# Attention with key-block summaries and a two-branch max layer: 128 key rows of one padded k per query tile, v loaded by token and spread by engine copies, max layer in units of 256 tokens

## The chip, the cores and the metric

The kernel runs on one core of a Trainium2 chip. The metric is the device time of one execution in microseconds (us); lower is better. The core has a matrix engine (TensorE, PE in the profile, with its weight loads as PEld), a vector engine (VectorE, DVE), a scalar engine (ScalarE, ACT), a general engine (GpSimd, POOL) and a queue that issues the transfers of this kernel (SyncE, SP). Matrix products land in PSUM, which has eight banks here; everything else lives in SBUF, 128 partitions wide.

## The reference

Four batches, eight heads, 768 tokens, head size 64. Each query sees the keys nearer than 16 tokens and, besides, 24 summaries of blocks of 32 tokens (key: the maximum over the block; value: the mean), all in one softmax. The result, 3072 tokens of width 512, goes through a layer that takes the larger of two projections and projects it back.

```python
def _attn_ref(q, k, v):
    ...
    k_sum = k.reshape(B, H, nb, block, D).max(axis=3)
    v_sum = v.reshape(B, H, nb, block, D).mean(axis=3)
    scores_l = scale * np.matmul(q, k.transpose(0, 1, 3, 2))
    mask_l = np.abs(pos[:, None] - pos[None, :]) < window
    scores_s = scale * np.einsum('bhsd,bhnd->bhsn', q, k_sum) + np.log(block)
    a = softmax(concat([where(mask_l, scores_l, -1e9), scores_s]))
    return a @ concat([v, v_sum])

def _moe_ref(x, w1, w2, w_out):
    g = np.maximum(x @ w1, x @ w2)
    return g @ w_out
```

(The two formulas are shortened here to what is computed.) The maximum is rewritten as x@w1 + relu(x@(w2−w1)), so the kernel needs the difference of the weights (`wd`), `w_out` (`wo`), and the product w1@w_out (`w1o`), which it makes once.

## The kernel before, in words

Queries are cut into 12 tiles of 64 tokens per batch. A tile sees a window of 96 keys (at most) and the 24 summaries: NK = 120 rows. Two heads are worked on at once (a head pair `hp`, four in a batch) and three groups `grp` of four tiles.

`load_batch` (L137) issues for each head pair one load of k, q and v, 384 KB each, in which a descriptor is 512 B (two tokens of one head). `load_weights` (L144) issues twelve loads of 512 KB. All transfers are issued from the SP queue, in its order; the stage tiles of k, q and v have three buffers each.

`prep_v` (L179) casts v to bf16 on DVE (L182, `vb`), then spreads it with 16 SBUF-to-SBUF transfers (L188 to L195) into `vext`, which holds for each tile the 96 value rows of its window, and makes the 24 means with six matmuls (L199, `vs_ps`), copies them once (L201) and repeats them over the tiles with one more transfer (L202). `prep_kq` (L207) casts k and q on DVE (L211, L213), transposes them on PE (L219), copies the windows of k on DVE (L231, L232), takes the block maxima (L234, `ks`), repeats them with one POOL copy (L236) into `kext`, and copies q on ACT (L242) into a block-diagonal `qbd`. `scores` (L246) does four matmuls (L253), an exponential on ACT (L255) into one of four `prob` buffers, and a mask product on DVE (L262). `values` (L266) does the matmuls with `vext` (L277) and, for every three tile pairs, a reciprocal (L282) and a product (L284) on DVE; the accumulator `av` has one PSUM buffer. `transpose_x` (L288) transposes the result (L294) and copies it on DVE (L296) into `xt`, in halves of 384 tokens.

`maxout` (L323) takes a half: eight hidden tiles of four matmuls with 384 columns (L330), a relu on ACT (L332), and three output tiles of twelve matmuls with 512 columns (L339, L343), an ACT copy (L347) and a store. The output accumulator `o_ps` has one PSUM buffer.

The program (L352 on) is: load batch 0, prepare its v, load the weights, attention of batch 0 alone, cast the weights (`cast_weights`, L157: `w1b` L160, `wd` L161 on DVE, `wo` L162 on ACT), make `w1o` (L164); then for each batch the max layer of batch b woven step by step with the attention of batch b+1. The order in which each engine and the SP queue take their instructions is not that of the text: the framework plans it ahead, instruction by instruction, from its own estimates of durations, the earlier in the text the sooner among what it takes to be ready. On the chip each engine then follows that fixed order, and waits wherever an instruction's operands are late.

The softmax here doesn't subtract the row's maximum and nothing guards it: scores larger than these inputs give would overflow.

## Time and profile before

| what | value |
|---|---|
| median of two runs | 225.51 us (224.62 and 226.40) |
| the profiled execution | 225.93 us, span 224.2 us |
| granted TensorE clock, mean | 0.985 |
| PE busy | 174.6 us (78%), 1475 matmuls |
| DVE busy | 118.0 us (53%) |
| ACT busy | 102.7 us (46%) |
| POOL busy | 23.9 us (11%) |
| transfers | 37.68 MB in 49858 packets |

The span is what the engines' records cover; the profiled execution's own time is 1.7 us longer. Busy shares are means over stages with different limits, so the profile is read by stretches of time: the start (load, attention of batch 0), the middle (max layer of one batch beside attention of the next), and the end (the max layer of batch 3 alone). In the lists, L is a line of the kernel printed above; a row of the list of groups gives the shapes as output<-input, a count, the busy time and the mean duration in ns.

### The profile page before, as it was taken

Reading aid. Unit: us, or ns where it says so; the run is one execution under the profiler, and the core shown is the slowest. Engines: PE = TensorE matmul, PEld = TensorE weight load, DVE = VectorE, ACT = ScalarE, POOL = GpSimd, SP = SyncE. Lnnn points to the kernel's source line nnn. Section 1 sums busy time; section 2 is a strip of 40 time slices with the busy share of each in tenths; the row PEclk is TensorE's granted clock in tenths of the full one; section 3 lists DMA queues with packets and bytes.
Section 4 is the critical chain, followed back from the end, with each engine's and each line's share of the span. In section 5 each row is a group of like instructions: output and inputs, shape, how many; then the busy total and the mean of one; then the engine's idle time right before and its main releaser. Section 6 shows DMA issues by size and latency. Waiting matters only on the chain.

```text
span 224.2 us, 3831 instructions
## 1 busy us (share of the span) xinstructions
PE 174.6 (78%) x1475; PEld 103.8 (46%) x1496; DVE 118.0 (53%) x268; ACT 102.7 (46%) x173; POOL 23.9 (11%) x61
## 2 busy tenths in 40 slices
PE   0003832665788999896989999999999999999973
PEld 0001622543553655664555466655546664544531
DVE  5432852899972950896857069844727853000000
ACT  2000651575120573585179248824935972442521
POOL 8990110000000010000011001000000000000000
PEclk9999999997699999999999999999999999999999
DMA  6998438999997335999634599634431101202112
GB/s 187 289 290 273 106 100 251 375 365 283 288 281 183 90 90 135 288 292 282 184 117 102 158 259 306 163 116 152 103 87 50 51 0 47 96 0 95 47 47 94
DMA packets 49858, 37.68 MB, mean 168 GB/s; under 512 B 2192, under 2 KB 44720, under 8 KB 49840
## 3 DMA queue, kind: packets, MB, share of 16 engines
q1 hardware_dynamic: 49840, 37.45, 58.5%
q8 instruction: 11, 0.18, 0.3%
q14 instruction: 7, 0.06, 0.1%
HBM read 25.17 MB, written 6.29 MB: 140 GB/s over the span
## 4 chain that ended last, share of the span: by engine, by line
PE 49%; DMA 15%; DVE 13%; ACT 11%; SPq 7%; issue 3%; POOL 1%; ACTq 0%; POOLq 0%
PE o_ps L343 16%; DMA vf<-in_v_dram 13%; PE h_ps L330 11%; PE o_ps L339 8%; PE av L277 4%; PE sc L253 2%; ACT g L332 2%; PE x_ps L294 2%; DMA vext_115<-vext_115 2%; DVE wd L161 2%; SPq L127 2%; ACT qbd_107 L242 2%; PE vs_ps L199 2%; ACT qbd_108 L242 2%; PE w1o_ps L174 2%
## 5 line engine op out<-in xcount | busy, mean ns | idle before, releaser
L330 PE MATMUL h_ps<-xt,wd 128*128 128x384 bf16 x256 | 54.2, 331 | 2.5 <-DVE xt L296 1.1
L343 PE MATMUL o_ps<-wo,g 128*128 128x512 bf16 x186 | 46.5, 379 | 0.3
L332 ACT ACTIVATE g<-h_ps 128x384 bf16<-128x384 f32 x64 | 30.1, 491 | 15.7 <-PE h_ps L330 15.2
L347 ACT COPY osb<-o_ps 128x512 f32<-128x512 f32 x24 | 14.1, 586 | 49.2 <-PE o_ps L343 49.1
L330 PEld LDWEIGHTS <-wd 128*128 128x128 bf16 x256 | 23.7, 98 | 16.8 <-issue 3.0
L343 PEld LDWEIGHTS <-g 128*128 128x128 bf16 x192 | 17.9, 98 | 18.2
L339 PE MATMUL o_ps<-w1o,xt 128*128 128x512 bf16 x83 | 24.1, 378 | 2.1 <-ACT osb L347 1.4
L199 PE MATMUL vs_ps<-vb_113,amean 128*128 128x512 bf16 x12 | 4.2, 502 | 20.4 <-DVE vb_113 L182 20.4
L282 DVE RECIPROCAL inv<-av 128x6 f32<-128x6 f32 x32 | 6.1, 190 | 25.0 <-PE av L277 24.9
L284 DVE TENSOR_TENSOR x<-av,inv 128x384 bf16<-128x384 f32 x32 | 17.6, 550 | 0.3
L234 DVE TENSOR_REDUCE ks<-k_ps 128x24 bf16<-128x768 bf16 x16 | 15.1, 945 | 0.0
L162 ACT CAST wo<-wof 128x1024 bf16<-128x1024 f32 x4 | 4.2, 1043 | 23.8 <-DMA wof<-in_moe_w_out_dram 23.8
L339 PEld LDWEIGHTS <-xt 128*128 128x128 bf16 x96 | 9.1, 97 | 10.4 <-issue 4.0
L199 PEld LDWEIGHTS <-amean 128*128 128x128 bf16 x24 | 2.5, 107 | 24.3 <-issue 13.8
L296 DVE COPY xt<-x_ps 128x384 bf16<-128x384 bf16 x32 | 11.3, 352 | 2.8 <-PE x_ps L294 2.2
L294 PE MATMUL x_ps<-identity,x 128*128 128x128 bf16 x96 | 11.2, 230 | 1.4 <-ACT qbd_108 L242 0.6
L242 ACT COPY qbd_107<-q_ps 64x768 bf16<-64x768 bf16 x10 | 7.9, 792 | 9.3 <-PE q_ps L219 9.2
L255 ACT ACTIVATE prob_109<-sc,bias 120x512 bf16<-120x512 f32 x12 | 8.3, 689 | 7.8 <-PE av L277 6.7
L242 ACT COPY qbd_106<-q_ps 64x768 bf16<-64x768 bf16 x12 | 9.5, 793 | 4.0 <-PE q_ps L219 3.9
L213 DVE CAST qb<-qf 128x768 bf16<-128x768 f32 x16 | 10.3, 647 | 1.1 <-DMA qf<-in_q_dram 1.1
L182 DVE CAST vb_113<-vf 128x768 bf16<-128x768 f32 x8 | 5.1, 638 | 10.4 <-DMA vf<-in_v_dram 10.3
L219 PE MATMUL k_ps<-identity,kb 128*128 128x128 bf16 x96 | 9.8, 236 | 1.0 <-DVE ks L234 0.9
(94 smaller groups left out, 251.0 us busy)
## 6 DMA issues: line engine op xcount, KB each, us to landing
kf<-in_k_dram SPq DMA_DIRECT2D x16, 384.0 KB
qf<-in_q_dram SPq DMA_DIRECT2D x16, 384.0 KB
vf<-in_v_dram SPq DMA_DIRECT2D x16, 384.0 KB
out_dram<-osb SPq DMA_DIRECT2D x24, 256.0 KB
w1f<-in_moe_w_dram SPq DMA_DIRECT2D x4, 512.0 KB
wof<-in_moe_w_out_dram SPq DMA_DIRECT2D x4, 512.0 KB
w2f<-in_moe_w_dram SPq DMA_DIRECT2D x4, 512.0 KB
vext_115<-vb_113 SPq DMA_DIRECT2D x8, 148.5 KB
```

Of the source, the lines that this page charges most:

```text
L199: nc.tensor.matmul(out=ps[:], lhsT=amean[:, c, :], rhs=vbt[:, c, j, :, 0:D], start=(c == 0 and j == 0), stop=(c == 2 and j == 1))
L213: nc.vector.tensor_copy(out=qb[:], in_=by_slot(loads["qf", b, hp]))
L234: nc.vector.tensor_reduce(out=ks[:], in_=kps.rearrange("p j (n g) -> p n j g", g=16), axis=AX.XY, op=ALU.max)
L242: nc.scalar.copy(out=qx[r, :, a * 64:a * 64 + 64].rearrange("p t (g j) -> p t g j", j=2), in_=qps[r].rearrange("p j (t g) -> p t g j", g=32))
L284: nc.vector.tensor_tensor(out=x[:], in0=av[:, :, :, 0:D], in1=inv[:].to_broadcast([128, 3, 2, D]), op=ALU.mult)
L294: nc.tensor.transpose(out=ps[:, u, :], in_=xs[half][:, u].rearrange("p a d -> p (a d)"), identity=identity[:])
L296: nc.vector.tensor_copy(out=xts[b, half][:, hp, :], in_=ps[:].rearrange("p u n -> p (u n)"))
L330: nc.tensor.matmul(out=h[:], lhsT=wd[:, c, f * 128:f * 128 + 128], rhs=xt[:, c, :], start=(c == 0), stop=(c == KC - 1))
L332: nc.scalar.activation(out=g[:, f, :], in_=h[:], func=ACT.Relu)
L339: nc.tensor.matmul(out=ps[:], lhsT=xt[:, c, sl], rhs=w1o[:, c, :], start=(c == 0), stop=False)
L343: nc.tensor.matmul(out=ps[:], lhsT=g[:, f, sl], rhs=wo[:, f, :], start=False, stop=(f == FC - 1))
L347: nc.scalar.copy(out=o[:, u, :], in_=ps[:])
```

## The change

The mask rows are rearranged and the geometry is made uniform. k is kept once per head pair as a padded row of 96 columns per tile (64 keys, 24 maxima, 8 zeros), and a tile's matmul reads 128 columns of it: its own 96 and the first 32 of the next tile. So K is 128 in place of 120 and one mask of 64 columns serves all tiles. `qbd` is laid out by head instead of by tile.

v is loaded by token: ten transfers per batch, with descriptors of 256 B (one token of one head), into one f32 tile `vf` with 128 tokens to a row block; it is cast into one bf16 tile `vb` (on POOL), and eight engine copies (on DVE in batch 0, on POOL later) spread it to `vext`, with a shift of partitions. The means are seven matmuls; the copy over the tiles is a DVE copy in batch 0 and a transfer later. The copy of the maxima goes from POOL to DVE.

The max layer works on three groups of 256 tokens in place of two halves of 384: four relu's of 512 columns per group, and one PSUM tag `mm` with two buffers for hidden and output tiles; `av` gets two buffers, `prob` nine. The transposes of the attention result are done for two head pairs at once. Weights are loaded in halves of the hidden width, w1 and w2 ahead of the loads of batch 1, w_out among them. For batch 0 there are an own attention (`first_attention`: casts of k on POOL and of q on ACT for head pairs 1 to 3, casts on DVE for k of pair 0, a third of the mask products on POOL) and an own max layer (`first_maxout`: half of the hidden tiles first, then the w1 transposes and `w1o`), which is woven with the attention of batch 1. `pin` keeps the marked instructions in program order.

```diff
-    NK = 96 + nb
...
+    NG, GT = 3, 256
+    KW = 96 * NT + 32
+    NV, VW = 7, 66
+    NBUF, NPB, WFB = 3, 9, 8
...
-    kext = [const.tile([128, NT, 128], BF16, name=f"kext{i}") for i in range(NBUF)]
-    qbd = [const.tile([128, NT, 128], BF16, name=f"qbd{i}") for i in range(NBUF)]
-    NPB = 4
-    prob = [const.tile([128, 8 * 128], BF16, name=f"prob{i}") for i in range(NPB)]
+    kext = [const.tile([128, KW], BF16, name=f"kext{i}") for i in range(NBUF)]
+    qbd = [const.tile([128, 2, S], BF16, name=f"qbd{i}") for i in range(NBUF)]
+    prob = [const.tile([128, 4, 192], BF16, name=f"prob{i}") for i in range(NPB)]
+    vf = const.tile([128, NV, H, D], F32, name="vf")
+    vb = const.tile([128, NV, H, D], BF16, name="vb")
+    vext = [const.tile([128, NT, H, VW], BF16, name=f"vext{i}") for i in range(2)]
+    mask = const.tile([128, 64], BF16, name="mask")
...
+    def fixed(i):
+        nc.vector.memset(qbd[i][0:64, 1], 0.0)
+        nc.vector.memset(qbd[i][64:128, 0], 0.0)
+        sums = kext[i][:, 0:96 * NT].rearrange("p (t c) -> p t c", c=96)[:, :, 88:96]
+        nc.gpsimd.memset(sums, 0.0)
+        nc.gpsimd.memset(kext[i][:, 0:16], 0.0)
+        nc.gpsimd.memset(kext[i][:, KW - 16:KW], 0.0)
...
+    for i in range(NPB):
+        nc.vector.memset(prob[i][:, :, 64:128], 0.0)
...
+    def load_v(b):
+        nc.sync.dma_start(out=vf[16:128, 0], in_=v[b, :, 0:112].rearrange("h r d -> r h d"))
+        for h in range(H):
+            nc.sync.dma_start(out=vf[:, 1:NV - 1, h], in_=v[b, h, 112:752].rearrange(
+                "(m r) d -> r m d", r=128))
+        nc.sync.dma_start(out=vf[0:16, NV - 1], in_=v[b, :, 752:768].rearrange("h r d -> r h d"))
...
+    def load_w(w, n):
+        for c in (0, 2):
+            t = stage.tile([128, 2, 512], F32, tag="wf", bufs=WFB, name="wf")
+            if w < 2:
+                nc.sync.dma_start(out=t[:], in_=wview[w][:, c:c + 2, n * 512:n * 512 + 512])
+            else:
+                nc.sync.dma_start(out=t[:], in_=wview[w][:, 4 * n + c:4 * n + c + 2, :])
+            wload[w, n, c] = t
...
+    def cast_w12(n):
+        sl = slice(n * 512, n * 512 + 512)
+        w1b[n] = work.tile([128, KC, 512], BF16, tag="osb", bufs=2, name="w1b")
+        for c in (0, 2):
+            w1f, w2f = wload[0, n, c], wload[1, n, c]
+            pin(nc.vector.tensor_tensor(out=wd[:, c:c + 2, sl], in0=w2f[:], in1=w1f[:],
+                                        op=ALU.subtract))
+            pin(nc.gpsimd.tensor_copy(out=w1b[n][:, c:c + 2], in_=w1f[:]))
+
+    def cast_wo(n):
+        for c in (0, 2):
+            pin(nc.scalar.copy(out=wo[:, 4 * n + c:4 * n + c + 2, :], in_=wload[2, n, c][:]))
...
-    def prep_v(b):
...
+    def cast_v(b, eng):
+        eng.tensor_copy(out=vb[:, 0:NV - 1], in_=vf[:, 0:NV - 1])
+        eng.tensor_copy(out=vb[0:32, NV - 1], in_=vf[0:32, NV - 1])
+
+    def spread_v(b, engines):
+
+        vx = vext[b % 2]
+        for a, eng in enumerate(engines):
+            for t0, r0, m0 in ((0, 0, 0), (1, 64, 0)):
+                eng.tensor_copy(
+                    out=vx[0:64, t0:NT:2, 4 * a:4 * a + 4, 0:D],
+                    in_=vb[r0:r0 + 64, m0:m0 + 6, 4 * a:4 * a + 4, :])
+            for t0, r0, m0 in ((0, 64, 0), (1, 0, 1)):
+                eng.tensor_copy(
+                    out=vx[96:128, t0:NT:2, 4 * a:4 * a + 4, 0:D],
+                    in_=vb[r0:r0 + 32, m0:m0 + 6, 4 * a:4 * a + 4, :])
+
+    def mean_v(b, by_dma):
+        vx = vext[b % 2]
+        ps = psum.tile([128, H, D], F32, tag="mm", bufs=2, name="vs_ps")
+        for m in range(NV):
+            nc.tensor.matmul(out=ps[:].rearrange("p h d -> p (h d)"), lhsT=amean[:, m, :],
+                             rhs=vb[:, m].rearrange("p h d -> p (h d)"),
+                             start=(m == 0), stop=(m == NV - 1))
+        s = slice(64, 96)
+        nc.vector.tensor_copy(out=vx[s, 0, :, 0:D], in_=ps[s])
+        (nc.sync.dma_start if by_dma else nc.vector.tensor_copy)(
+            out=vx[s, 1:NT].rearrange("p t h w -> p t (h w)"),
+            in_=vx[s, 0:1].rearrange("p t h w -> p t (h w)").to_broadcast([32, NT - 1, H * VW]))
...
+    def cast_kq(b, hp, k_on, q_on):
+        r = []
+        for tag, eng in (("kf", k_on), ("qf", q_on)):
+            t = work.tile([128, 6, 2, D], BF16, tag=tag[0] + "b", bufs=2, name=tag[0] + "b")
+            (eng.copy if eng is nc.scalar else eng.tensor_copy)(out=t[:], in_=by_slot(loads[tag, b, hp]))
+            r.append(t)
+        kqb[b, hp] = r
...
     def prep_kq(b, hp):
...
+        kt = kx[:, 0:96 * NT].rearrange("p (t c) -> p t c", c=96)
+        nc.vector.tensor_copy(
+            out=kt[:, 1:NT, 0:64].rearrange("p t (g j) -> p t g j", j=2),
+            in_=kps[:, 24:376].rearrange("p (t g) j -> p t g j", g=32))
+        nc.vector.tensor_copy(out=kt[:, 0, 16:64].rearrange("p (g j) -> p g j", j=2),
+                              in_=kps[:, 0:24])
+        nc.vector.tensor_copy(
+            out=kx[:, 96 * NT:96 * NT + 16].rearrange("p (g j) -> p g j", j=2),
+            in_=kps[:, 376:384])
+        ks = work.tile([128, nb], BF16, tag="ks", bufs=2, name="ks")
+        nc.vector.tensor_reduce(out=ks[:], in_=pss[0][:].rearrange("p j (n g) -> p n j g", g=16),
+                                axis=AX.XY, op=ALU.max)
+        nc.vector.tensor_copy(out=kt[:, :, 64:64 + nb],
+                              in_=ks[:].rearrange("p (o n) -> p o n", o=1).to_broadcast(
+                                  [128, NT, nb]))
+        for a in range(2):
+            r = slice(a * 64, a * 64 + 64)
+            nc.scalar.copy(out=qx[r, a, :].rearrange("p (g j) -> p g j", j=2), in_=qps[r])
...
+    def scores(b, hp, grp, mask_on=nc.vector):
+        i = (b * NP + hp) % NBUF
+        kx, qx = kext[i], qbd[i]
+        pb = prob[(3 * (b * NP + hp) + grp) % NPB]
+
+        sc = psum.tile([128, 2, 2, 2, 64], F32, tag="sc", bufs=2, name="sc")
+        for i in range(4):
+            t = 4 * grp + i
+            nc.tensor.matmul(out=sc[:, i // 2, :, i % 2], lhsT=kx[:, 96 * t:96 * t + 128],
+                             rhs=qx[:, :, 64 * t:64 * t + 64], start=True, stop=True)
+        pv = pb[:, :, 0:128]
+        pv = bass.AP(pv.tensor, pv.offset, [pv.ap[0], pv.ap[1], [128, 2], [1, 64]])
+        nc.scalar.activation(out=pv, in_=sc[:].rearrange("p i a w q -> p (i a) w q"),
+                             func=ACT.Exp, bias=bias[:], scale=scale)
+        mk = mask[:].rearrange("p (i o q) -> p i o q", i=1, o=1).to_broadcast([128, 4, 2, 64])
+        mask_on.tensor_tensor(out=pv, in0=pv, in1=mk, op=ALU.mult)
...
     def values(b, hp, grp):
...
+        av = psum.tile([128, 2, 2, D + 1], F32, tag="av", bufs=2, name="av")
...
+        if hp == 0:
+            xts[b, grp] = work.tile([128, KC, GT], BF16, tag="xt", bufs=6, name="xt")
+        if hp % 2:
+            ps = psum.tile([128, 2, 2, 128], BF16, tag="tr", bufs=2, name="x_ps")
+            for p in range(2):
+                for u in range(2):
+                    nc.tensor.transpose(out=ps[:, p, u, :],
+                                        in_=xs[b, grp][:, p, u].rearrange("p a d -> p (a d)"),
+                                        identity=identity[:])
+            nc.vector.tensor_copy(out=xts[b, grp][:, hp - 1:hp + 1, :],
+                                  in_=ps[:].rearrange("p h u n -> p h (u n)"))
...
     def attention(b):
+        cast_kq(b, 0, nc.vector, nc.vector)
+        prep_kq(b, 0)
+        yield
+        for hp in range(NP):
+            if hp + 1 < NP:
+                cast_kq(b, hp + 1, nc.vector, nc.vector)
+            scores(b, hp, 0)
+            yield
+            scores(b, hp, 1)
+            yield
+            if hp + 1 < NP:
+                prep_kq(b, hp + 1)
+                yield
+            values(b, hp, 0)
+            yield
+            scores(b, hp, 2)
+            yield
+            values(b, hp, 1)
+            yield
+            values(b, hp, 2)
+            yield
...
+    def hidden(b, grp, fps):
+        xt = xts[b, grp]
+        for fp in fps:
+            h = psum.tile([128, 2, GT], F32, tag="mm", bufs=2, name="h_ps")
+            for s in range(2):
+                f = 2 * fp + s
+                for c in range(KC):
+                    nc.tensor.matmul(out=h[:, s, :], lhsT=wd[:, c, f * 128:f * 128 + 128],
+                                     rhs=xt[:, c, :], start=(c == 0), stop=(c == KC - 1))
+            nc.scalar.activation(out=gs[grp][:, 2 * fp:2 * fp + 2, :], in_=h[:], func=ACT.Relu)
+            yield
...
+        for u in range(2):
+            ps = psum.tile([128, d_model], F32, tag="mm", bufs=2, name="o_ps")
...
+    def maxout(b):
+        for grp in range(NG):
+            yield from hidden(b, grp, range(4))
+            yield from output(b, grp)
+
+    def prepared(b):
+        a = attention(b)
+        for _ in range(3):
+            yield next(a)
+        cast_v(b, nc.gpsimd)
+        spread_v(b, (nc.gpsimd, nc.gpsimd))
+        yield
+        mean_v(b, True)
+        yield from a
...
+    def first_attention():
+        for hp in range(NP):
+            cast_kq(0, hp, nc.gpsimd if hp else nc.vector, nc.scalar)
+            prep_kq(0, hp)
+            for grp in range(NG):
+                scores(0, hp, grp, nc.gpsimd if grp == 2 else nc.vector)
+            if hp == 0:
+                cast_v(0, nc.gpsimd)
+            if hp == 1:
+                spread_v(0, (nc.vector, nc.vector))
+                mean_v(0, False)
+            if hp == 3:
+                cast_w12(0)
+            if hp >= 2:
+                for grp in range(NG):
+                    values(0, hp - 2, grp)
+        for hp in (2, 3):
+            for grp in range(NG):
+                values(0, hp, grp)
+
+    def first_maxout():
+        for grp in range(NG):
+            yield from hidden(0, grp, (0, 1))
+        cast_w12(1)
+        yield from transpose_w1(0)
+        for grp in range(NG):
+            yield from hidden(0, grp, (2, 3))
+        cast_wo(0)
+        cast_wo(1)
+        yield from transpose_w1(1)
+        yield from make_w1o()
+        for grp in range(NG):
+            yield from output(0, grp)
...
+    load_kq(0, 0)
+    load_kq(0, 1)
+    load_v(0)
+    load_kq(0, 2)
+    load_kq(0, 3)
+    for n in range(2):
+        load_w(0, n)
+        load_w(1, n)
+    first_attention()
+    ones(1)
+    load_kq(1, 0)
+    load_v(1)
+    load_w(2, 0)
+    load_kq(1, 1)
+    load_w(2, 1)
+    load_kq(1, 2)
+    load_kq(1, 3)
+    for b in range(B):
+        side = iter(())
+        if b + 1 < B:
+            if b:
+                load_v(b + 1)
+                for hp in range(NP):
+                    load_kq(b + 1, hp)
+            side = prepared(b + 1)
+        weave(maxout(b) if b else first_maxout(), side, 1.0)
```

## Prediction

> **What bounds the kernel now.** I read the 40 slices first, then busy times by stretch, then the chain and the longest waits, and at last the start instruction by instruction. (About 2% is what a measurement of this kernel can tell from no change.)
>
> ```profile
> PE   0003832665788999896989999999999999999973
> DVE  5432852899972950896857069844727853000000
> DMA  6998438999997335999634599634431101202112
> ```
>
> PE is nearly full from the eleventh slice (60 us) on and nearly empty before. The stretches say it in microseconds: start and end, busy time (instructions) of PE, PEld, DVE, ACT, POOL, then clock, transfer share and GB/s.
>
> ```profile
> 12.00:20.00 8.00, 0.00 (x0) 0.00 (x0) 1.55 (x3) 0.00 (x0) 4.33 (x10) 1.00 1.14 311
> 20.00:33.00 13.00, 8.83 (x55) 5.95 (x55) 8.81 (x17) 6.74 (x9) 1.16 (x2) 1.00 0.43 122
> 33.00:40.00 7.00, 1.93 (x26) 1.61 (x26) 2.41 (x6) 1.38 (x2) 0.00 (x0) 1.00 0.77 235
> 40.00:60.00 20.00, 12.89 (x154) 9.50 (x154) 18.51 (x43) 10.73 (x15) 0.86 (x2) 0.84 1.02 331
> 60.00:85.00 25.00, 23.25 (x165) 12.88 (x167) 15.63 (x33) 8.90 (x17) 1.05 (x2) 0.99 0.66 170
> ```
>
> PE does 23.7 us in the first 60 us; from 60 to 220.8, where the last matmul ends, the windows sum to 151.0 of 160.8 us. So the middle and the end are bound by PE, and the start by something else:
>
> ```profile
> PE vs_ps L199 <- DVE vb_113 L182: 20.4, 1, 20.4
> PE av L277 <- DMA vext_115<-vext_115: 4.1, 1, 4.1
> ...
> 4.20 1.00 DVE L211 CAST kb<-kf 128x768 bf16<-128x768 f32 x1 [1.11 <-DMA kf<-in_k_dram]
> 19.74 0.56 DVE L182 CAST vb_113<-vf 128x768 bf16<-128x768 f32 x1 [3.45 <-DMA vf<-in_v_dram]
> 32.18 0.82 SPq L202 DMA_DIRECT2D vext_115<-vext_115  x1
> 33.05 0.53 SPq L154 DMA_DIRECT2D w2f<-in_moe_w_dram  x1
> ```
>
> Keys are on hand at 4.2 us, but PE's first matmul in its fixed order is that of the means, which waits until 20.4 us for all of v. The SP queue then issues 17 spreads, the last at 32.2 us; nine of the twelve weight loads stand behind it, so transfers fall to 0.43 of their capacity from 20 to 33 us and the weights end after 50 us. The first values wait for the last spread until 36.8 us.
>
> **The middle, in PE time.** The chain lists 24 hidden matmuls of 384 columns in 4.08 us and 8 output ones in 1.74 us, thus 163 and 216 ns apart. Eight of 128 columns take 0.61 us (57 ns apart), eight av ones 0.41 us (30 ns). Per batch: attention 96 × 57 (k, q, scores) + 24 × 57 + 96 × 30 + 6 × 216 ns = 11.0 us, max layer 64 × 163 + 72 × 216 ns = 26.0 us; w1 and w1o once 32 × 57 + 32 × 216 ns = 8.7 us.
>
> **The change part by part.**
>
> *PE work.* Hidden: 96 matmuls of 256 columns per batch; between the rows of 128 (57 ns) and 384 (163) lies 110 ns, so 10.6 us against 10.4 (0.13 more, unrounded). Means: one more, 0.22 us. Over four batches +1.4 us; at the end, two buffers for o_ps remove the waits of PE on the ACT copy (two of 0.67 to 0.72 us): −1.4. K = 128 for 120 rows moves no column: 0; at most the 8 more rows in 120 if rows counted, 7% of 2.9 us.
>
> *The start, transfers.* Four k/q loads come first; today's fourth load is on hand at 8.95 us. v is then 6144 descriptors of 256 B, 384 to an engine. In the transfer records of the trace a 512 B packet takes 31 ns (median), one of 1056 B 52, one of 2048 B 86; drawn down to 256 B that is 21.5, and no more than 31. I take 26, nearer to the 512 B row: 10.0 us (8.3 to 11.9), v lands at 18.9. The other k/q loads take 4 × 1.35 us (384 KB at 292 GB/s): 24.3; eight weight loads of 512 KB 14 us: the first half at 31, the second at 38. No issue in the SP queue waits for an engine's late result any more: the 17 spreads are gone from it in batch 0 (one is left later), ten v issues replace four, and weights stand behind inputs only. Beside that, the ten v issues at today's 0.43 to 1.3 us lie within their own transfer time.
>
> [...]
>
> *The start, v chain.* POOL casts 3072 elements: its casts of 128 and 512 elements take 281 and 608 ns, so 0.17 us + 0.85 ns each: 2.8 us, and 0.6 for the small piece: 22.3 us. The spread on DVE is 8 copies of 1536 bf16. The nearest row is the f32 SBUF cast of 1024 in 687 ns, 0.52 ns each above a fixed 0.15 us; half of that at best for half the bytes, 1 ns (the reduction's rate) at worst, for the shift of partitions is in no row. I take 0.39, between the cast's rate and its half: 0.75 us each, 6.0 us (4.4 to 13). The mean's copy 0.7 and its repeat over 5808 elements 2.4 (1.7 to 6).
>
> [...]
>
> *The start, DVE.* From 22.3 us DVE has before it, besides those 9.1: k of pairs 2 and 3, each about 1.05 (copies: 704, 48 and 16 elements by the k copy's 0.52 to the reduction's 1.04 ns) + 0.945 (maxima) + 0.3 (their repeat, 288 elements): 4.6; four masks of 0.42: 1.7; twelve reciprocals of 0.19 and twelve products of 256 elements (0.55 us at 384, so 0.42): 7.3; six xt copies of 512 (0.42): 2.5; two wd halves of 1.21: 2.4. That is 27.6 us, ending at 49.9. The last two groups and the waits for them (2 to 3 us) lie beside hidden matmuls of the first group, as today's attention ends at 60 with 2.5 us of later PE work done. So today's 60 becomes **47** (41 to 54). The cover for PE's own 14 us of the start is this DVE queue; without it, PE would be the next late one.
>
> *The middle, the port.* POOL takes over cast and spread for batches 1 to 3: 15.9 thousand elements in 10 instructions, 15.6 us a batch by its rows, hidden behind some 40 us of PE. But POOL and DVE hold each other up:
>
> ```profile
> 9.12 0.63 POOL L83 CAST mask<-m_72 128x128 bf16<-128x128 f32 x1
> 10.31 1.22 DVE L213 CAST qb<-qf 128x768 bf16<-128x768 f32 x1 [0.70 <-DMA qf<-in_q_dram]
> L211 DVE CAST kb<-kf x16: 515/550/999, 4.2 to 162.2; 128x768 bf16<-128x768 f32 x16
> L236 POOL COPY kext_104<-ks x5: 429/561/694, 28.3 to 162.5; 128x288 bf16<-128x288 bf16 x5
> ```
>
> The same POOL cast takes 281 ns alone and 630 beside a DVE cast; the qb cast takes 1.22 us for 0.55 beside a POOL memset. Each side seems to wait for the other's whole instruction. DVE has 24 such operations a batch (8 casts, 12 masks, 4 repeats), its quiet sum is 29.1 us by the rows above (28.5 today), and ten POOL instructions can each hold one up by 0.7 to 1.1 us: 36 to 40 us, level with PE. POOL's 15.6 becomes 20 to 27. I charge 2 us in all (−4, for two av buffers and smaller units, to 12).
>
> v of batch 1 lands near 51 us (38 + 2.7 + 10), POOL needs until 71 to 78 and the repeat 2 more. Until then PE has max layer 0, w1o and the scores of batch 1, some 40 us from 47 on: covered to about 87. If the planned order puts the values of batch 1 earlier, PE stalls up to 10 us there.
>
> *Sum.* 47 + 160.8 + 1.4 − 1.4 + 2 = 209.8; then 3.4 to the span's end as today (last ACT copy, store) and 1.7 around it: **215**. The profiled execution has 225.93, so −11; the median of the runs is 225.51, 0.4 below it.
>
> **Rivals.** (1) *The means stay ahead on PE.* Today's order put them before the k transposes. If it does again, k copies begin only at 22.3 us and DVE has all its k work and masks after it, some 8 us more: 47 becomes 55, the time 223. Against it: in the changed text two head pairs precede them. (2) *POOL becomes the bound, and it is slower than before.* Batch 3's v is spread at 51 + 3P; then values (10), max layer 3 (26.5) and 5.1: 93 + 3P exceeds 230 from P = 46 us a batch, 2.9 ns an element. For it: the contended cast above (4.9 ns an element at 128), an affine select of 192 elements in 672 ns (3.5), a shift of partitions that no row shows. Against it: contended kext copies at 694 ns for 288 elements are 2.4. At 3.1 ns it gives 236. (3) *DVE copies fast and the start ends at 40:* 208. (4) *The change does not shorten the start, since weights bind:* wd's second half is needed only 20 us of PE work after 47 and lands at 38; little chance.
>
> **How the numbers follow.** Forecast 0.66 (own range 208 to 221), fast start 0.08, means ahead 0.13 (218 to 228), POOL or port bound 0.13 (225 to 245, nine tenths of it slower). Range 202 to 228, which leaves out most of rival 2 and a tail below. Faster by over 2% (under 221): forecast, fast start and a little of rival 1 less the forecast's tail, 0.72; within 2%: 0.16; slower: 0.12.
>
> **What would show it.** Transposes of k on PE before 8 us; the start's transfers at 0.9 or more up to 38 us; first values at 32 to 36 and xt of group 0 at 45 to 47; POOL 75 to 100 us busy, its spread copies 1.5 us alone; qb casts and masks with more long cases; bytes down to 33 MB (6.0 MB of spreads less 1.1 that stay). Wrong it would be if av in the middle waits for vext, if DVE exceeds 95% in any 40 us, or if PE's gaps between 50 and 90 us sum to over 8 us.

## The result, and the profile after

The changed kernel takes **239.2 us** (median of 238.91 and 239.49), against 225.51 before: 1.0607 times as long, 95% interval 1.0419 to 1.0796. The forecast was 215, range 202 to 228. The profiled execution of it has a span of 237.8 us (before 224.2) and a mean granted clock of 0.889 (before 0.985).

The 40 slices of the changed kernel, as in the prediction's first fence, with POOL and the granted TensorE clock beside them:

```profile
PE   0267237329935569999999957999999999999994
DVE  7547998997676793995007999584772864600000
POOL 7319101899900899000000898000000000000000
PEclk9999857755985556999999997999999999999998
DMA  7999999499069940194664560511106011112112
```

A slice is 5.9 us here. PE does start early (second and third slice), and transfers are dense from the second slice on, as the change promised. But PE then falls back twice, from the fifth to the ninth slice and again from the twelfth to the fifteenth (65 to 89 us), where before it was full from the eleventh (60 us) on. The clock is at half in parts of the first of these stretches and in most of the second. (The clock is on record only from 24.6 us on here, and from 43.3 us on in the kernel before; ahead of that the profile shows full clock for want of a record. Eight score matmuls take 1.06 us at 12.35 us here and 1.02 at 26.34 before, where the prediction's row at full clock has 0.61, so both starts ran slow, and the two mean clocks, 0.889 and 0.985, cannot be set side by side. From 60 us on they can.) The same stretches as in the prediction, with the same columns (start and end, busy time and instructions of PE, PEld, DVE, ACT and POOL, then clock, transfer share, GB/s):

```profile
20.00:33.00 13.00, 5.11 (x30) 2.99 (x29) 12.79 (x13) 3.83 (x5) 4.48 (x5) 0.81 1.07 370
33.00:40.00 7.00, 4.90 (x64) 4.37 (x64) 6.55 (x21) 3.42 (x5) 1.15 (x1) 0.62 1.17 212
40.00:60.00 20.00, 11.51 (x124) 9.02 (x122) 17.84 (x32) 3.83 (x6) 17.47 (x12) 0.66 0.87 248
60.00:85.00 25.00, 15.12 (x137) 11.73 (x137) 17.72 (x32) 15.48 (x23) 11.83 (x9) 0.68 0.85 169
```

From 60 to 85 us PE is busy 15.1 of 25 us, at 0.68 of its clock; before, it was busy 23.3 at 0.99. That is the stretch where the result was decided. By 60 us PE had been busy for 27.2 us, against 23.7 before, part of it at half clock in both; so little was gained in the start, and the middle lost it many times over.

The events behind it are in the order of time of all engines (start, duration, engine, line, operation; in brackets the engine's idle time before it and who ended that):

```profile
33.64 0.54 PE L292 MATMUL av<-vext_89,prob_78 128*128 128x65 bf16 x7 [3.91 <-DVE vext_89 L216]
...
47.04 2.74 POOL L191 CAST vb<-vf 128x3072 bf16<-128x3072 f32 x1
...
47.12 3.07 DVE L230 CAST kb<-kf 128x768 bf16<-128x768 f32 x1
...
50.53 1.95 DVE L230 CAST qb<-qf 128x768 bf16<-128x768 f32 x1
...
74.30 3.87 ACT L165 CAST wo<-wf 128x1024 bf16<-128x1024 f32 x4
...
75.85 1.01 PE L172 MATMUL w1t_ps<-identity,w1b 128*128 128x128 bf16 x8 [2.23 <-DVE w1t L174]
...
81.07 1.03 PE L274 MATMUL sc<-qbd_75,kext_72 128*128 128x128 bf16 x8 [2.66 <-DVE kext_72 L259]
...
83.64 4.34 DVE L159 TENSOR_TENSOR wd<-wf 128x1024 bf16<-128x1024 f32 x2
...
84.53 4.76 POOL L203 COPY vext_89<-vb 32x1536 bf16<-32x1536 bf16 x2
...
85.63 1.04 PE L349 MATMUL h_ps<-xt,wd 128*128 128x256 bf16 x4 [0.59 <-DVE wd L159]
88.03 4.24 PE L349 MATMUL h_ps<-xt,wd 128*128 128x256 bf16 x19 [1.36 <-DVE wd L159]
```

Two things are to be seen. First, a DVE cast that takes 0.55 us takes 3.07 beside POOL's cast of v, and ends 0.4 us after that; the next one takes 1.95 beside POOL's first spread copy. Secondly, the second half of `wd` is made at 83.64 us, although its weights had been in SBUF for 50 us (the last of these loads is issued before 23 us, and none takes over 10.9 to land): DVE takes it right behind the last product of the first values of batch 1 (at 83.30): `cast_w12(1)` stands behind those steps in the program, and DVE's planned order has it there too. Until then PE has used up the first half of the hidden tiles (the last of them at 65.6 us), and nothing is left to fill the waits of the attention of batch 1 and of the w1 transposes, which it runs through alone from 65 to 85 us. The hidden matmuls from 88.03 on run at a granted clock of 0.50 for four more microseconds, some 210 ns apart (19 start in 4 us), where at full clock later 32 of them take 3.5 us, 109 ns apart.

So there are two theories. **A, the late weights:** what costs is the place of `cast_w12(1)`. **B, the port:** what costs is that POOL now works beside DVE in every batch, each holding the other up. ("Port" is the author's name for it: the runs show that the two engines hold each other up, and not what they share.) They can be told apart, since either can be undone alone.

### The profile page after: what moved, and what is told of

It is laid out like the page before. It is cut to its first block, busy times and chain, and to the rows that moved or that the text cites. A ratio compares the mean times of both kernels' runs of the same rounds, so it can differ in the third digit from the quotient of the medians.

```text
span 237.8 us, 4143 instructions
## 1 busy us (share of the span) xinstructions
PE 183.1 (77%) x1628; PEld 124.8 (53%) x1628; DVE 146.8 (62%) x318; ACT 104.7 (44%) x161; POOL 70.6 (30%) x76
## 5 line engine op out<-in xcount | busy, mean ns | idle before, releaser
L349 PE MATMUL h_ps<-xt,wd 128*128 128x256 bf16 x384 | 53.3, 291 | 4.5 <-DVE wd L159 3.3
L349 PEld LDWEIGHTS <-wd 128*128 128x128 bf16 x384 | 38.4, 104 | 12.5 <-DVE wd L159 4.1
L351 ACT ACTIVATE g<-h_ps 128x512 bf16<-128x512 f32 x48 | 28.3, 598 | 32.0 <-PE h_ps L349 31.7
L191 POOL CAST vb<-vf 128x3072 bf16<-128x3072 f32 x4 | 11.0, 2744 | 57.5 <-DMA qf<-in_q_dram 36.2
L242 PE MATMUL k_ps<-identity,kb 128*128 128x128 bf16 x96 | 10.3, 247 | 13.6 <-POOL vext_90 L112 7.1
L300 DVE TENSOR_TENSOR x<-av,inv 128x256 bf16<-128x256 f32 x48 | 20.1, 420 | 0.8
L308 PE MATMUL x_ps<-identity,x 128*128 128x128 bf16 x96 | 13.7, 233 | 3.5 <-DVE x L300 2.4
L257 DVE TENSOR_REDUCE ks<-k_ps 128x24 bf16<-128x768 bf16 x16 | 15.2, 948 | 0.0
L311 DVE COPY xt<-x_ps 128x512 bf16<-128x512 bf16 x24 | 10.1, 422 | 6.4 <-PE x_ps L308 6.4
L199 POOL COPY vext_90<-vb 64x1536 bf16<-64x1536 bf16 x8 | 12.3, 1539 | 0.3
L242 PE MATMUL q_ps<-identity,qb 128*128 128x128 bf16 x96 | 10.9, 259 | 1.6 <-DVE qb L230 1.4
L203 POOL COPY vext_90<-vb 32x1536 bf16<-32x1536 bf16 x8 | 12.0, 1502 | 0.4
L230 DVE CAST kb<-kf 128x768 bf16<-128x768 f32 x13 | 11.5, 885 | 0.1
```

Source lines behind the costliest of these rows:

```text
L199: eng.tensor_copy(out=vx[0:64, t0:NT:2, 4 * a:4 * a + 4, 0:D], in_=vb[r0:r0 + 64, m0:m0 + 6, 4 * a:4 * a + 4, :])
L203: eng.tensor_copy(out=vx[96:128, t0:NT:2, 4 * a:4 * a + 4, 0:D], in_=vb[r0:r0 + 32, m0:m0 + 6, 4 * a:4 * a + 4, :])
L230: (eng.copy if eng is nc.scalar else eng.tensor_copy)(out=t[:], in_=by_slot(loads[tag, b, hp]))
L242: nc.tensor.transpose(out=ps[:, j, 128 * c:128 * c + 128], in_=src[:, 2 * c + j].rearrange("p h d -> p (h d)"), identity=identity[:])
L257: nc.vector.tensor_reduce(out=ks[:], in_=pss[0][:].rearrange("p j (n g) -> p n j g", g=16), axis=AX.XY, op=ALU.max)
L300: nc.vector.tensor_tensor(out=xs[b, grp][:, hp % 2], in0=av[:, :, :, 0:D], in1=inv[:].to_broadcast([128, 2, 2, D]), op=ALU.mult)
```

## The experiments

All are the changed kernel ("after") or the kernel before with one edit, timed against the kernel before on the same chip.

| kernel | us | ratio to before, 95% interval | PE busy, us | PE idle up to its last matmul, us |
|---|---|---|---|---|
| before | 225.51 | 1 | 174.6 | 46.1 |
| after | 239.2 | 1.0607 [1.0419, 1.0796] | 183.1 | 51.1 |
| 1 after, `wd` early | 228.91 | 1.0182 [1.0127, 1.0237] | 175.2 | 48.4 |
| 2 after, v off POOL | 229.26 | 1.0169 [1.0137, 1.0202] | 180.0 | 43.5 |
| 3 after, both | 219.97 | 0.9752 [0.9716, 0.9789] | 173.9 | 41.0 |
| 4 before, no maxima on POOL | 223.3 | 0.99 [0.9863, 0.9938] | 174.5 | 43.1 |
| 5 the same, idle POOL copies | 230.19 | 1.0222 [1.0142, 1.0302] | 177.9 | 46.6 |
| 6 as 3, start's POOL work gone | 214.69 | 0.9525 [0.948, 0.9571] | 172.1 | 37.2 |
| 7 as 6, `wd` behind batch 0's values | 214.49 | 0.9512 [0.9466, 0.9557] | 174.4 | 35.4 |
| 8 before, means later | 236.7 | 1.0476 [1.0405, 1.0548] | 175.9 | 56.1 |
| 9 the same, weights behind means | 225.11 | 1.0 [0.9973, 1.0026] | 176.5 | 44.6 |
| 10 before, units of 256 | 229.13 | 1.0178 [1.0129, 1.0227] | 179.2 | 43.7 |
| 11 the same, evicted in pairs | 225.54 | 1.0026 [0.9995, 1.0057] | 178.4 | 40.8 |

Busy and idle are of one profiled execution each. A PE busy time that grows with the same instructions points to a slower clock (hidden matmuls 210 ns apart at a granted 0.50, 109 at full clock): after and kernel 3 issue the same 1628 matmuls, and differ by 9.2 us there. (Of kernels 6 and 7 the trace holds 1609 of 1628 matmuls, so their busy time is a little low and their idle time a little high.)

**1. The weights' place alone.**

```diff
 # first_attention
             if hp == 3:
                 cast_w12(0)
+                cast_w12(1)
 # first_maxout
-        cast_w12(1)
```

> The changed kernel with the casts of the second weight halves of w1 and w2 moved in the text from behind the first half of the hidden tiles to right behind the casts of the first halves (and pinned there). Theory A (the second half of wd is pinned behind the values of batch 1, so PE runs out of hidden tiles between 65 and 88 us): PE busy from 65 to 88 us rises from about 13 to at least 18 us and the time falls from 239 to 222 to 230 us. Theory B (DVE is held up by POOL's casts and copies through a shared port, wherever the weights are cast): the time stays at 234 us or more, and the gaps of PE only move.

Measured 228.91 us: 10.3 us of the 13.7 lost come back. In the stretch where PE had its trough, and in the order of time:

```profile
60.00:85.00 25.00, 21.17 (x239) 15.83 (x238) 19.74 (x46) 20.14 (x30) 11.14 (x8) 1.00 0.66 142
```

```profile
68.46 1.15 PE L349 MATMUL h_ps<-xt,wd 128*128 128x256 bf16 x9
...
74.95 1.91 PE L349 MATMUL h_ps<-xt,wd 128*128 128x256 bf16 x16
```

PE is busy 21.2 of 25 us, at full clock: hidden matmuls of the second half now lie between the steps of batch 1's attention. By the table, 7.9 of the gain is a shorter PE busy time and only 2.7 less idling. The clock record goes with that: 30.9 us of PE's busy time lie at a granted 0.50 in the changed kernel and 12.7 in kernel 1, and half of the difference is 9.1. So most of the cost of the late weights shows as matmuls at half clock. This is a way of booking it, and no run separates it further: a slow matmul that fills a wait adds to the busy time and takes as much from the idle time. The edit has a price of its own: all four `wd` pieces now stand ahead of batch 0's last values on DVE and take 7.3 us there, beside POOL's casts, so that PE is busy only 8.8 us from 40 to 60 (11.5 in the changed kernel).

**2. The port alone.** The cast of v for batches 1 to 3 goes to ACT, its spread to DVE; POOL has nothing left to do there.

```diff
-        cast_v(b, nc.gpsimd)
-        spread_v(b, (nc.gpsimd, nc.gpsimd))
+        cast_v(b, nc.scalar)
+        spread_v(b, (nc.vector, nc.vector))
```

> The changed kernel with v of batches 1 to 3 cast on ACT and spread on DVE (about 0.56 us a copy as in batch 0) in place of POOL. Theory A: the pinned wd cast still stands behind the values of batch 1, which now come some 10 us earlier: 230 to 238 us. Theory B: DVE's casts, masks and wd differences run at their quiet times (0.55, 0.42, 1.21 us) after 50 us, and the time falls to 226 us or less.

Measured 229.26 us, 9.9 us less than after, though DVE has been given 24 copies more. That is below what A alone had for it (230 to 238) and above what B alone had (226 or less): each has a part. The window and the `wd` piece:

```profile
60.00:85.00 25.00, 15.09 (x133) 11.47 (x131) 20.51 (x46) 16.56 (x22) 0.00 (x0) 0.73 0.64 130
```

```profile
80.56 2.35 DVE L159 TENSOR_TENSOR wd<-wf 128x1024 bf16<-128x1024 f32 x2
```

The trough is still there, as theory A wants it with `wd` still at 80.6 us; but the two pieces take 2.35 us instead of 4.34. What is gained lies for the larger part in the idle time (7.6 us less by the table, and 3.1 less busy).

The edit also puts the copies on an engine that makes one in 0.56 us where POOL takes 1.46 or more, so a POOL that was merely too slow would be a rival. The trace speaks against it: the last spread copy of batch 1's v ends at 62.9 us in the changed kernel and at 68.5 in kernel 2, so v is ready later there, and the kernel is faster all the same. And the changed kernel shows a hold on its way to PE, beside the spread of batch 3's v:

```profile
138.54 1.68 DVE L281 TENSOR_TENSOR prob_86<-prob_86,mask 128x512 bf16<-128x512 bf16 x1
...
140.14 1.68 DVE L281 TENSOR_TENSOR prob_78<-prob_78,mask 128x512 bf16<-128x512 bf16 x1
...
141.74 1.68 DVE L281 TENSOR_TENSOR prob_79<-prob_79,mask 128x512 bf16<-128x512 bf16 x1
...
144.14 0.62 PE L292 MATMUL av<-vext_89,prob_86 128*128 128x65 bf16 x8 [4.25 <-DVE x L300]
```

Three masks of 0.42 us take 1.68 each, the product behind them comes late, and PE waits 4.25 us for it. In kernel 2 no wait of the values for a product is longer than 1.2 us.

**3. Both.** The edits of 1 and 2 together.

> Both edits: weights cast early and v of batches 1 to 3 off POOL. If A and B are separate causes the gains add: 212 to 222 us, under the kernel before. If one is the other's consequence, e3 is within 3 us of the better one of the two.

Measured 219.97 us: 19.2 us less than after, against 10.3 + 9.9 = 20.2 for the two alone. The gains add up but for 1 us, so the two causes are separate, and without them the change is faster than before.

**4 and 5. The port in a kernel that is otherwise unchanged.** Kernel 4 is the kernel before, with the repeat of the maxima on DVE, so that POOL is silent after the start. Kernel 5 adds five POOL copies a head pair in batches 1 to 3, 60 in all, into a tile that nobody reads: work without a use, so that only its side effect is timed.

```diff
-        nc.gpsimd.tensor_copy(out=kx[:, :, 96:NK],
+        nc.vector.tensor_copy(out=kx[:, :, 96:NK],
 # kernel 5 besides
+        for _ in range(5 if b else 0):
+            nc.gpsimd.tensor_copy(out=spare[:], in_=ks[:].rearrange(
+                "p (o n) -> p o n", o=1).to_broadcast([128, 32, nb]))
```

> The kernel before with one part of the change alone: the repeat of the key maxima (288 elements) on DVE in place of POOL. It is the base for the next run. Both theories: within 2 us of the kernel before (225.5), since DVE gains 16 x 0.23 us and one hand-over per head pair falls away.

> The run e4 with, in batches 1 to 3, five POOL copies of 768 bf16 elements per head pair that nobody reads (60 in all, about 0.8 us each, about 16 us a batch, as much POOL time as the changed kernel's cast and spread of v). Theory B (the port alone costs the time): DVE's casts and masks show many durations above 0.8 us and the time grows by 5 us or more against e4. Theory A (the order of the weights is what costs): DVE slows where it overlaps, but PE has work in hand, and the time grows by less than 2 us.

Measured 223.3 and 230.19 us: nothing but idle POOL copies costs 6.9 us. The group of kernel 5, and the same DVE cast as above (count: min/median/max ns):

```profile
L242 POOL COPY spare<-ks 128x768 bf16<-128x768 bf16 x60 | 56.7, 944 | 115.2 <-DVE ks L236 78.3 <-DVE inv L287 33.7
```

```profile
L213 DVE CAST kb<-kf x16: 544/550/1173, 4.2 to 164.4; 128x768 bf16<-128x768 f32 x16
```

DVE is busy 136.9 us in place of 117.5: 0.32 us more for each POOL copy, 0.94 us long. The test is a clean one: in the two traces PE, ACT and DVE take the same instructions in the same order, and nothing waits for the idle copies. Of the 19.4 us by which DVE is longer busy, 6.9 reach the time. Kernel 4 by itself is 2.2 us below before (within 2 was expected). That is about 1% for taking the maxima from POOL, one part of the change; but the planned orders on PE and DVE differ from those of before as well, so it is not POOL's silence alone.

**6 and 7. The start without POOL.** Kernel 6 is kernel 3 with the last POOL work of batch 0 (three casts of k, four masks, the cast of v) on DVE and the casts of `w1b` on ACT. Kernel 7 puts `cast_w12(1)` behind all of `first_attention()` in kernel 6.

```diff
-            pin(nc.gpsimd.tensor_copy(out=w1b[n][:, c:c + 2], in_=w1f[:]))
+            pin(nc.scalar.copy(out=w1b[n][:, c:c + 2], in_=w1f[:]))
-            cast_kq(0, hp, nc.gpsimd if hp else nc.vector, nc.scalar)
+            cast_kq(0, hp, nc.vector, nc.scalar)
-                scores(0, hp, grp, nc.gpsimd if grp == 2 else nc.vector)
+                scores(0, hp, grp, nc.vector)
-                cast_v(0, nc.gpsimd)
+                cast_v(0, nc.vector)
 # kernel 7 besides
-                cast_w12(1)
     first_attention()
+    cast_w12(1)
```

> The run e3 (weights cast early, v of batches 1 to 3 off POOL) with POOL taken out of the start too: batch 0's k casts, mask products and v cast on DVE, the w1 casts on ACT. If the port holds DVE up in the start as in the middle (in e3 two masks take 3.81 us for 0.84, four wd differences 7.26 for 4.84), the last xt copy of batch 0 comes at 50 to 53 us in place of 56, and the time falls from 220 to 213 to 217 us. If the start is bound by the amount of DVE's work, the added 7 us on DVE (3 casts, 4 masks, the v cast) cancel it: 219 to 223 us.

> The run e6 with the second weight halves cast behind the attention of batch 0 instead of in its middle. If they stand in the way of batch 0's values there (2 x 1.21 us on DVE), 1.5 to 3 us less than e6; if PE has other work then, the same as e6 within 1 us.

Measured 214.69 and 214.49 us. The first is 5.3 us less than kernel 3: the start paid for the port as well, although DVE took over some 5.5 us of work (the edit also moves `w1b` to ACT, and no run takes that apart). The second is no gain, where 1.5 to 3 us were expected: the last copy into `xt` comes at 51.1 us in place of 53.6, but PE then waits for ACT, which has the cast of batch 1's v (2.75 us from 51.22 on) and two copies of q in front of the relu that is waited for:

```profile
56.15 0.82 PE L350 MATMUL h_ps<-xt,wd 128*128 128x256 bf16 x6 [3.02 <-ACT g L352]
```

Both are faster than before and after, and their times do not tell them apart. The quiet cast, in the changed kernel and in kernel 7:

```profile
L230 DVE CAST kb<-kf x13: 534/551/3069, 6.5 to 177.5; 128x768 bf16<-128x768 f32 x13
```

```profile
L231 DVE CAST kb<-kf x16: 529/552/560, 6.5 to 153.4; 128x768 bf16<-128x768 f32 x16
```

With POOL silent, none of 16 casts takes over 0.56 us; beside POOL's work the longest takes 3.07.

**8 and 9. What bound the start before.** The prediction had PE wait for v with its first matmul until 20.4 us, and behind that the spreads in the SP queue. Kernel 8 is the kernel before with the means of batch 0 taken after the first scores, so that k goes first on PE. In kernel 9 `load_weights()` is moved behind the means too.

```diff
-    load_weights()          # kernel 9: moved
-    for _ in attention(0):
+    first = attention(0)
+    for _ in range(3):
+        next(first)
+    mean_v(0)
+    load_weights()          # kernel 9
+    for _ in first:
         pass
```

> The kernel before with one part alone: the six matmuls of batch 0's means moved in the text behind the preparation and the first two score groups of head pair 0. If the wait of 20.4 us for v on PE is what holds the start, 6 us or more are gained (below 219.5). If the spreads in the SP queue end later (first values at 36.8 us) and cover it, the time moves by less than 3 us although PE starts before 10 us.

> The kernel before, its means for batch 0 taken behind the scores of pair 0 (as in the run with later means), and the weight loads written behind the means, so that the repeat of the means no longer stands behind weight loads in the SP queue. If the wait of PE for v at 20.4 us sets the start of the kernel before (the prediction's first step), k work done early now pays: first values 2 to 5 us earlier than 36.75, time 219 to 223. If the last transfer into the values' tile sets it, first values stay near 36 and the time is 224 to 227, and the 237 of the run with later means was the place of that transfer in the queue. If weights bind the start, loads issued some us later cost more than the earlier values bring: 227 or more, with the wait of the hidden matmuls for the weights in the trace.

Kernel 8 took 236.7 us, kernel 9 225.11. The first missed both theories' numbers, since it had moved more than was meant: the repeat of the means now stood behind ten weight loads in the SP queue. (In the kernel before it stood ahead of ten; two of the twelve went ahead of the spreads, so the prediction's nine is one short.)

```profile
41.32 0.83 SPq L205 DMA_DIRECT2D vext<-vext  x1
...
50.39 0.76 PE L280 MATMUL av<-vext,prob 120*128 120x65 bf16 x11 [22.41 <-DMA vext<-vext]
```

Kernel 9 mends that. PE starts at 5.2 us instead of 20.4, and yet:

```profile
32.71 0.82 SPq L205 DMA_DIRECT2D vext<-vext  x1
...
37.34 0.76 PE L280 MATMUL av<-vext,prob 120*128 120x65 bf16 x11 [8.32 <-DMA vext<-vext]
```

The first values come at 37.3 us (before 36.75), and the time is that of before within 0.3%. So the early start of PE, as far as it goes here, gained nothing: the start was set by the last transfer into `vext`, behind 16 spreads in the SP queue, and a place ten issues later cost 11 us. It does not go far: twelve transposes run from 5.2 us on, and then the scores wait 10.8 us, until 17.77, for POOL's copy of the maxima. The first weight load behind the spreads is issued at 33.58 us in place of 33.05, so the run does not say what later weights would cost.

**10 and 11. The max layer in units of 256 alone.** Kernel 10 is the kernel before with three groups of 256 tokens for two halves of 384. Kernel 11 evicts two hidden tiles at once, as the change does.

```diff
-                h = psum.tile([128, 384], F32, tag="h", bufs=2, name="h_ps")
+                h = psum.tile([128, 256], F32, tag="h", bufs=2, name="h_ps")      # kernel 10
+                h = psum.tile([128, 2, 256], F32, tag="h", bufs=2, name="h_ps")   # kernel 11
...
+            nc.scalar.activation(out=g[:, 2 * fp:2 * fp + 2, :], in_=h[:], func=ACT.Relu)
```

> The kernel before with its max layer in units of 256 tokens in place of 384 (values, transposes, hidden and output tiles alike), all else as before: this part of the change alone. The prediction has 0.13 us a batch for the hidden matmuls and some gain for smaller units: 222 to 226. If the smaller units themselves are part of the loss (more evictions on ACT, more waits of PE for them), 228 or more.

> The kernel before in units of 256 tokens, as in the run before it, but with two hidden tiles of 256 columns in one PSUM tile and one ACT eviction of 512 elements for both, which is the form of the change. In the run with one eviction for each 256 columns, 24 hidden matmuls at the end took 3.10 us (129 ns apart) where the changed kernel has 32 in 3.5 (109 ns). If the eviction of small tiles was what cost the 4 us, the spacing falls to 110 ns and the time to 223 to 226. If the smaller units themselves cost it, 228 or more.

Measured 229.13 and 225.54 us. Hidden matmuls at the end of kernel 10, then of kernel 11:

```profile
195.56 2.74 PE L330 MATMUL h_ps<-xt,wd 128*128 128x256 bf16 x20
198.35 0.38 PE L339 MATMUL o_ps<-w1o,xt 128*128 128x512 bf16 x1
```

```profile
191.66 3.24 PE L332 MATMUL h_ps<-xt,wd 128*128 128x256 bf16 x26
194.74 1.03 PE L343 MATMUL o_ps<-w1o,xt 128*128 128x512 bf16 x4
```

From start to start that is 2.79 us for 20, 139 ns apart, and 3.08 for 26, 118 apart; in the changed kernel it is 109. Small units cost nothing if their evictions stay large; evicted one by one they cost 4 us. (For kernel 11 a spacing of 110 was expected; the time came as expected.) The change has the large evictions, so this part of it, on the kernel before, is neutral.

## Why the prediction was wrong

**The step that failed is the one from holds to time in the port term** (a hold is the time by which a POOL instruction makes a DVE one longer). "I charge 2 us in all (−4 … to 12)." Measured: 9.9 us for batches 1 to 3 (kernel 2) and 5.3 for the start (kernel 6, which also moves `w1b`), together 15. The holds were in the prediction ("Each side seems to wait for the other's whole instruction"), and so, nearly, was their size: DVE's quiet 29.1 us a batch were to become 36 to 40, thus 7 to 11 more. In the changed kernel DVE is busy 146.8 us and in kernel 2 140.1, of which 13.4 are the 24 copies that it has besides; so the holds of three batches are some 20 us, 6.7 a batch. They were fewer and longer than the "0.7 to 1.1 us" of the prediction's rows: 0.55 us grew to 1.95 and 3.07, and a mask of 0.42, held through four POOL instructions in a row, to 3.47. What was wrong is that 20 us of holds could be had for 2 us of time, since PE had "some 40 us" of work as cover and DVE was only "level with PE". About half came through: 9.9 of some 20 us here, 6.9 of 19.4 in kernel 5. And the term was for batches 1 to 3 alone; the start, which the prediction had found to be bound by DVE, had POOL at work beside it (17.5 us from 40 to 60) and was priced by quiet rows.

**"So today's 60 becomes 47 (41 to 54)" failed.** The last `xt` copy is at 56.8 us. The queue of DVE that this step added up held only batch 0's work at quiet durations. On the chip, `kb` and `qb` of batch 1 stand in front of batch 0's last values and take 5.0 us (1.1 quiet), the first half of `wd` takes 3.3 (2.4 quiet), and the masks of the start are held as above. With POOL silent it is 51.1 (kernel 7), with DVE bearing some 5.5 us more work than the change gives it: of the 9.8 us by which the step was off, 5.7 are gone in that kernel, and 4.1 stay. So the step was nearer to right for the engine that it looked at, and had no term for what holds that engine up.

**The rival that was dismissed came true in another form.** Rival 4 said that `wd`'s second half "is needed only 20 us of PE work after 47 and lands at 38; little chance". The landing was no later than that (34 us at most). But a weight is not on hand when it lands, but when its cast has run, and that stood behind steps of batch 1: a thing that was to be read from the program, not from the profile. The place cost 10.3 us (kernel 1). The prediction came close elsewhere ("if the planned order puts the values of batch 1 earlier, PE stalls up to 10 us there") but looked at PE's queue alone, not at what is queued behind those values on DVE, and gave it no chance.

**The clock had no term at all.** 160.8 us were carried over from the old middle and end, all at full clock. After the change the clock is at half in large parts of the first 93 us, and the same matmuls take 9.2 us longer than in kernel 3. The carried term itself holds where the two causes are absent: from the last `xt` copy of kernel 7 (51.1) to its last matmul (209.8) it is 158.7 us.

**The sum, put right:** 215 less the 2 us charged for the port, plus 9.9, 5.3 and 10.3, is 238.5; measured 239.2. That it comes so near is in part luck: undone together, the first two causes in batches 1 to 3 are worth 19.2 and not 20.2 us. Without them it is 213, and kernel 7 has 214.5; there too two errors offset each other, a start 4.1 us later than 47 and a rest 2.1 us shorter than 160.8.

**Rival 2 had nearly the right time for a wrong reason** (225 to 245, through a POOL that gets done too late). POOL's cast and spread took 15.5, 17.0 and 15.7 us in the three batches, which is the quiet price (15.6; the prediction's own rows add up to 15.2) and not the 20 to 27 that the prediction made of it beside DVE; it was busy 70.6 us where 75 to 100 were expected. Batch 1's v was spread at 62.9 us, before the 71 to 78 that the prediction gave it, and no wait of the values for POOL's copies into `vext` stands in the list of waits. POOL was not too slow, it was in the way.

**What held.** k transposes on PE at 7.1 us (before 8). 256 B packets at 21 ns median, 23.6 mean (26 taken). First values at 33.6 (32 to 36). Spread copies on DVE 0.56 us (0.75 taken, 0.55 the lower bound), repeat of the means 3.2 (2.4 taken). Hidden matmuls of 256 columns 109 ns apart (110). Transfers 32.8 MB (33). Max layer in units of 256: ratio 1.0026 (none expected). What did not hold besides: `xt` of group 0 was complete at 54.1 us (45 to 47 expected). Of the signs of being wrong, one came out: PE's gaps between 50 and 90 us were to sum to under 8 us, and from 65 to 90 alone they are 11.5. DVE never exceeded 95% in any 40 us (93% at most): it was not full, and its delays cost time all the same. And the start was not, as the first reading had it, a matter of the means being first on PE: kernel 9 takes that away and gains nothing; it was the SP queue's last transfer into `vext`.

## What to carry to other kernels

Before moving work to an idle engine, ask what it will hold up: POOL's time was hidden, but its instructions held up those of DVE that read and write SBUF (a 0.55 us cast took up to 3.07). So add up the holds by the length of the new instructions, and price them by what waits behind each held instruction: that PE had as much work on average was no cover (9.9 of some 20 us of holds reached the time), and a DVE that was busy for 93% at most was none either. Work that fills gaps (here half of the hidden tiles) must be available when the gaps come; follow its last producer through the fixed order of its engine, not only its transfer. And in this kernel a patchy stretch on PE cost twice, once as idle time and again as matmuls at half clock in it and behind it (PE was busy 9.2 us longer than in kernel 3).

## What was not expected of the hardware

**POOL and DVE held each other up for whole instructions, but not where DVE reads PSUM.** The 0.55 us cast that starts 0.08 us after POOL's 2.74 us cast ends 0.41 us after it; held the other way, POOL's spread copies of 1.46 us take up to 2.36 beside `wd`. In the changed kernel DVE's casts (up to 3.07 us), masks (3.47), `wd` differences (2.48), the repeat of the maxima within SBUF (1.84) and a spread copy (1.50) are the ones that grow. Those that read PSUM keep their quiet time, beside POOL's work too: at the longest the maxima take 0.95 us, the window copies 0.89, the `xt` copies 0.43 and the reciprocals 0.18. Of the 48 products 15 overlap POOL's work, and the longest of all takes 0.43 us:

```profile
L300 DVE TENSOR_TENSOR x<-av,inv x48: 393/424/426, 35.0 to 207.4; 128x256 bf16<-128x256 f32 x48
```

What the holds can be worth in time the idle copies show: 6.9 us for 60 of them (kernels 4 and 5).

**The clock fell in a patchy stretch, not only in a long gap.** In the changed kernel it is 0.50 from 70 to 85 us, where PE is still busy 2.5, 2.5 and 3.5 us in the three stretches of 5 us. It changes at 28.02, 38.27, 45.09, 58.74, 68.98, 92.88, 144.08 and 147.49 us, all of them whole multiples of 3.41 us apart. In the 3.41 us ahead of each fall PE was busy for 0 to 23%, ahead of each return for 90% or more. In between, the clock stayed as it was: stretches of 26 to 72% left it at half from 69 to 89.5 us, stretches of 67% (at 38.3 us) and 85% (at 58.7) left it full. Ahead of the fall at 68.98 the longest single gap was 1.4 us. That is what one trace shows; what sets the clock no run tells.

**256 B descriptors cost less than those of 512 B:** 21 ns against 28 (medians, changed kernel). Per byte the short packets were dearer, by about half (12 against 18 bytes per ns at these medians). The load by token still was no loss to speak of at the start: POOL's cast of v begins at 16.75 us, where DVE's last cast of v began at 19.74 in the kernel before.

**A 16-bit copy on DVE ran at 0.56 us for 1536 elements, though it shifts partitions,** 0.36 ns each. The repeat of the means, 5808 elements read again and again from one row of 528, took 3.17 us, 0.55 ns each. POOL took at least 1.46 us for the same copy of 1536.
